# The rows of v of items 8 and 9 fetched two items later, in the step of their own value products

## Chip, cores, metric

The kernel runs on one core of a Trainium2 chip. The metric is the device time of one execution in microseconds (us).

## What is computed

Causal attention with a decay bias on 32 heads (4 batches of 8, 576 positions, head size 64), then a gated linear unit over the 2304 tokens with two more matrices behind it, then a soft mixture of 8 experts with 4 slots each:

```python
scores = scale * np.matmul(q, k.transpose(0, 1, 3, 2))
bias = -(cum[:, :, :, None] - cum[:, :, None, :])      # cum: running sum of max(s, 0)
scores = np.where(causal, -1e9, scores + np.minimum(bias, 0.0))
attn = softmax(scores)
x = (attn @ v), heads side by side                     # 2304 x 512
h = ((x @ w1) * (x @ w2)) @ w3 @ w_out                  # 2304 x 512
logits = h @ phi
slot_input = softmax over tokens(logits).T @ h
slot_out[e] = relu(slot_input[e] @ moe2_w1[e]) @ moe2_w2[e]
out = softmax over slots(logits) @ slot_out
```

All of it is float32; some matrices come as 64-bit floats and are converted on the chip ("words").

## The kernel before

**Items.** Attention is done in 40 items (ITEMS, L273). Items 0 to 7 are heads 0 to 7 with the query tiles 0 to 2, items 8 to 15 the same heads with the query tiles 3 and 4, items 16 to 39 the other heads with all five tiles. A block of tokens (BLK, L34) is 320 or 256 columns wide.

**Steps of an item.** att_steps (L646) writes the work of each step n: the scores of item n (att_scores, L330: products on TensorE into sc_ps, reduction by VectorE at L352, exponential by ScalarE at L357); in between, att_norm (L362, GpSimd) and the transposes (att_transpose, L374: pt_ps and ptd_ps on TensorE, copied to pt and ptd by ScalarE at L387 and L401) of item n-1; the fetches of what comes next; and, in even steps, the value products of the pair n-2 and n-1 (att_pv, L403: x_ps on TensorE at L110, copied at L434 and L435). Fetches for later items are issued in the list prep: v by att_values (L293) one item ahead, the decay rows by att_prep (L301) and q and k by att_fetch (L275) three and four items ahead.

**v.** One fetch brings the rows of v of a pair of heads and is made at the odd item; it serves both items of the pair. There are two buffers for v (VB = 2, L85), so a fetch waits until the value products of an earlier pair have read the buffer.

**Words.** The matrices w1 and w2 come as 64-bit words, 512 KB at a time, in 16 pieces named w12_i_e (fetch_words, L175; three buffers, NRAW = 3). ScalarE (L192) and VectorE (L195, L196, L199) convert each piece, then ScalarE (L223) and GpSimd (L224) split it for the GLU products (glu_half, L441: gl on TensorE at L447). Behind them come wot and w3t, which are multiplied with phi early (use_rows, L240).

**Order.** SyncE (SP) issues nearly all fetches, strictly in the order in which the program writes them, and stands at each until its buffer is free. The other engines run in orders that a scheduler makes when the program is built. weave (L685) mixes the lists of attention, GLU and words by their costs; a fetch counts nothing in it.

Of the kernel before, what the change touches and what calls it, by code (L numbers as in the profile page):

```python
# [22 lines left out]
B, H, S, D = 4, 8, 576, 64  # L23
# [24 lines left out]
def attn_glu_softmoe_kernel(  # L48
# [244 lines left out]
    def att_values(n, ap):  # L293
        h, tiles = ITEMS[n]
        if h % 2:
            vt = ap.tile([P, 9, 2, D], F32, tag="v", name=f"v_{n}", bufs=VB)
            nv = 2 * tiles[-1] + 1
            nc.sync.dma_start(vt[:, :nv], v[h // 2, :, :nv])
            hd[n]["v"] = hd[n - 1]["v"] = vt

    def att_prep(n, ap):  # L301
        h, tiles = ITEMS[n]
        t = hd[n]
        raw, q0, q1 = t["raw"], t["q0"], t["q1"]
        if n < NF32:
            rows = raw
        else:
            rows = ap.tile([P, 2, S], F32R, tag="qb", name=f"qb_{n}", bufs=QAB)
            qa = ap.tile([P, 2, S], F32R, tag="qa", name=f"qa_{n}", bufs=QAB)
        if n < NDIR:  # L310
            for a in range(2):
                nc.sync.dma_start(rows[64 + 2 * a : 66 + 2 * a, :, :q1].bitcast(F32), dec[a][h : h + 1, :, :, :q1])
        else:
            (nc.scalar if NF32 <= n < 24 else nc.sync).dma_start(rows[64:68, :, :q1].bitcast(F32), rows_d[h].rearrange("a b n t -> (a b) n t")[:, :, :q1])
        if n < NF32:
            t["mul"] = [rows[:68]]
            return
        rq, rk, qb = raw[:, 0], raw[:, 1], rows
        nc.vector.tensor_copy(qa[:, 0, q0:q1], rq[:, q0:q1])  # L319
        nc.scalar.dma_start(qb[0:64, 0, q0:q1].bitcast(F32), qa[0:64, 0, q0:q1].bitcast(F32))  # L320
        nc.vector.tensor_copy(qa[:, 1, :q1], rk[:, :q1])
        nc.gpsimd.tensor_tensor(  # L322
            out=qb[0:64, 1, :q1], in0=rk[0:64, :q1], in1=qa[0:64, 1, :q1].bitcast(F32), op=ALU.subtract
        )
        nc.gpsimd.tensor_tensor(  # L325
            out=qa[64:, 0, q0:q1], in0=rq[64:, q0:q1], in1=qa[64:, 0, q0:q1].bitcast(F32), op=ALU.subtract
        )
        t["mul"] = [qa, qb[:68]]

    def att_scores(n, i, ap):  # L330
        t, tiles = hd[n], ITEMS[n][1]
        if i == tiles[0]:
            t["nmax"] = sm.tile([P, 6], F32, tag="nmax", name=f"nmax_{n}")
            t["rsum"] = rsum_t[n % 3]
            if n >= H or n % 2 == 0:
                t["sc"] = ap.tile([P, 1600], F32, tag="sc", name=f"sc_{n}", bufs=SCB)
            else:
                t["sc"] = hd[n - 1]["sc"][:, 800:]
        nmax, rsum, mul = t["nmax"], t["rsum"], t["mul"]
        q0, r = QT[i]  # L340
        W = q0 + r

        r = P
        sc = t["sc"][:, 64 * i * i : 64 * i * i + W]
        cuts = [(0, W)] if W <= 512 else [(0, W // 2), (W // 2, W)]
        for m, (a, z) in enumerate(cuts):
            pp = psum("sg", f"sc_ps_{n}_{i}_{m}")
            for x in mul:
                nc.tensor.matmul(pp[:r, : z - a], x[:, 0, q0 : q0 + r], x[:, 1, a:z], start=x is mul[0], stop=x is mul[-1])  # L349
            m0 = S - P if i == 0 else S - W + a  # L350
            last = m == len(cuts) - 1
            nc.vector.tensor_tensor_reduce(  # L352
                out=sc[:r, a:z], in0=pp[:r, : z - a], in1=hd["mask"][:r, m0 : m0 + z - a], scale=-0.125,
                scalar=3.0e38 if m == 0 else nmax[:r, 5:6], op0=ALU.add, op1=ALU.min,
                accum_out=nmax[:r, i : i + 1] if last else nmax[:r, 5:6],
            )
        nc.scalar.activation(  # L357
            out=sc[:r, :W], in_=sc[:r, :W], func=AF.Exp, bias=nmax[:r, i : i + 1], scale=-1.0,
            accum_out=rsum[:r, i, 0:1],
        )  # L360

    def att_norm(n):  # L362
        t, tiles = hd[n], ITEMS[n][1]
        rinv = sm.tile([P, 5], F32, tag="rinv", name=f"rinv_{n}")
        span = slice(tiles[0], tiles[-1] + 1)
        nc.vector.tensor_reduce(out=rinv[:, span], in_=t["rsum"][:, span], axis=AX.X, op=ALU.add)
        nc.vector.reciprocal(rinv[:, span], rinv[:, span])  # L367
        for i in tiles:
            sc = t["sc"][:, 64 * i * i : 64 * i * i + sum(QT[i])]
            nc.gpsimd.tensor_scalar(  # L370
                out=sc, in0=sc, scalar1=rinv[:, i : i + 1], scalar2=1.0, op0=ALU.mult, op1=ALU.mult
            )

    def att_transpose(n, i, ap):  # L374
        t = hd[n]
        tiles = [j for j in ITEMS[n][1] if j]
        if i == tiles[0]:
            t["pt"] = ap.tile([P, 10, P], F32, tag="pt", name=f"pt_{n}", bufs=PTB)
            t["ptd"] = ap.tile([P, 5, 64], F32, tag="ptd", name=f"ptd_{n}", bufs=PTB)
        pt, ptd = t["pt"], t["ptd"]  # L380
        W = sum(QT[i])
        sc = t["sc"][:, 64 * i * i : 64 * i * i + W]
        tp = psum("tp", f"pt_ps_{n}_{i}")
        for j in range(i):
            nc.tensor.transpose(tp[:, j * P : (j + 1) * P], sc[:, j * P : (j + 1) * P], ident)  # L385
        p0, step = PT[i]
        t["turned", i] = nc.scalar.copy(  # L387
            out=pt[:, p0 : p0 + step * (i - 1) + 1 : step], in_=tp[:, : i * P].rearrange("p (j q) -> p j q", q=P)
        )
        if i == tiles[-1]:  # L390


            dg = psum("tp", f"ptd_ps_{n}")
            own = [j for j in ITEMS[n][1] if j] + [0] * (ITEMS[n][1][0] == 0)
            for k in [len(own) - 1, *range(len(own) - 2, -1, -1)]:
                j = own[k]
                c0 = max(0, 64 * j * j + sum(QT[j]) - P)
                p0 = 64 * k + (64 if j == 0 else 0)
                nc.tensor.transpose(dg[:, p0 : p0 + P], t["sc"][:, c0 : c0 + P], ident)  # L399
                t["diag", j] = k  # L400
            t["turned", "d"] = nc.scalar.copy(out=ptd[:, : len(own)].rearrange("p j q -> p (j q)"), in_=dg[:, 64 : 64 * len(own) + 64])  # L401
# [244 lines left out]
    def att_steps(ap):  # L646

        groups = [[] for _ in range(B + 1)]
        N = len(ITEMS)
        for n in range(N + 1):  # L650
            tiles = ITEMS[n][1] if n < N else ()
            old = [i for i in ITEMS[n - 1][1] if i] if 0 < n <= N else []
            sc = [(0.2 + 0.3 * i, lambda i=i, n=n: att_scores(n, i, ap)) for i in tiles]
            tr = [(0.2 + 0.3 * i, lambda i=i, n=n: att_transpose(n - 1, i, ap)) for i in old]
            norm = [(0, lambda n=n: att_norm(n - 1))] if 0 < n <= N else []
            prep = [(0, lambda n=n: att_values(n + 1, ap))] if n + 1 < N else []
            d = FAR if n + FAR < NF32 else 1 if NF32 <= n + 1 < N else 0
            if d:
                prep += [(0, lambda m=n + d: att_prep(m, ap))]
            d = FAR + 1 if n + FAR + 1 < NF32 else 2 if NF32 <= n + 2 < N else 0  # L660
            if d:
                prep += [(0, lambda m=n + d: att_fetch(m, ap))]
            blks = [k for k in range(2) if BLK[k][2][0] in ITEMS[n - 1][1]]
            pv = [(1.4, lambda n=n, k=k: att_pv(n - 2, k)) for k in blks] if n > 0 and n % 2 == 0 else []
            groups[min(B, max(0, (n - 1) // H))] += [
                *sc[:1], *norm, *sc[1:2], *prep, *sc[2:3], *tr[:1], *sc[3:4], *tr[1:2], *sc[4:], *tr[2:], *pv
            ]
        return groups

# [77 lines left out]
    with tc.tile_pool(name="att", bufs=1) as ap:  # L747
# [14 lines left out]
        hd["mask"] = mask  # L762
        hd["ap"] = ap
        att = att_steps(ap)
        decay_rows()
        for n in range(NDIR):
# [20 lines left out]
        def load(k):  # L787
            i = k // 2 - 1
            if FC <= i < N0:
                (sum_rows if k % 2 else use_rows)(*TODO[i])  # L790
            if k < 2 * N0:
                load_words(k, ap)
            if k + NRAW < 2 * N0:
                fetch_words(k + NRAW, ap)
# [8 lines left out]
        prep = [(1, lambda k=k: load(k)) for k in range(2 * N0 + 2)]  # L803
# [15 lines left out]
        for b in range(2, B):  # L819
            steps, late = glu_steps(b - 1, late)  # L820
            n = len(more) // (B - b)
# [309 lines left out]
```

## Time and profile before

| | |
|---|---|
| median of 3 runs | 555.44 us (553.01 to 556.08) |
| profiled execution | 556.72 us, of which the span from first to last instruction 554.9 us |
| TensorE (PE) busy | 519.0 us, 94% |
| VectorE (DVE) busy | 316.0 us, 57% |
| ScalarE (ACT) busy | 311.5 us, 56% |
| GpSimd (POOL) busy | 199.2 us, 36% |
| moved by DMA | 118.03 MB, mean 213 GB/s |
| mean granted TensorE clock | 0.977 |

The table reads as averages over stages that differ. Steps 8 to 12, of which the change speaks, run between about 43 and 85 us.

### The profile page before, as it was taken

To read this page: it belongs to the slowest core of one execution; us is meant where nothing else is said; L and a number is where in the kernel's file an instruction comes from. 1 tells how busy PE (TensorE), PEld (TensorE's weight loads), DVE (VectorE), ACT (ScalarE), POOL (GpSimd) and SP (SyncE) were. 2 spreads that over 40 slices of the span, in tenths; PEclk is the share of its full clock that TensorE was granted. 3 is DMA by queue.
4 is the path that set the end of the run, shared out by engine and by line. 5 is a ranking of instruction groups with operands and counts; after the bars stand their busy time and mean duration, and the time that the engine had idled before them with its cause. 6 is when DMAs were issued, how large, how long until landed. Compare 5 with 4: busy or idle time off the path is not lost.

```text
span 554.9 us, 11841 instructions
## 1 busy us (share of the span) xinstructions
PE 519.0 (94%) x4288; PEld 436.2 (79%) x4288; DVE 316.0 (57%) x966; ACT 311.5 (56%) x845; POOL 199.2 (36%) x247
## 2 busy tenths in 40 slices
PE   3899799999889999999999899999999999999993
PEld 2667588888778898999989799898989999853452
DVE  7568677789865383866457677446641311243433
ACT  4576667688876674865687577557743211321222
POOL 5474463628764474343433444334220000000000
PEclk9997979999799999999999999999999999999998
DMA  5766953977572251654657347454403999689977
GB/s 153 246 164 181 284 186 135 305 289 252 180 254 98 77 189 40 206 174 154 194 170 231 128 150 222 130 170 131 153 33 119 406 409 388 238 297 424 420 288 242
DMA packets 38809, 118.03 MB, mean 213 GB/s; under 512 B 4224, under 2 KB 10560, under 8 KB 35296
## 3 DMA queue, kind: packets, MB, share of 16 engines
q1 hardware_dynamic: 36768, 113.60, 59.7%
q10 hardware_dynamic: 1984, 3.69, 2.5%
q8 instruction: 34, 0.56, 0.4%
q14 instruction: 23, 0.19, 0.1%
HBM read 102.11 MB, written 11.60 MB: 205 GB/s over the span
## 4 chain that ended last, share of the span: by engine, by line
PE 74%; DMA 9%; DVE 8%; issue 3%; ACT 2%; SPq 1%; POOL 1%; DVEq 0%; ACTq 0%; POOLq 0%
PE gl L447 33%; PE x_ps L110 8%; PE sc_ps L349 8%; PE pt_ps L385 5%; DMA raw_w<-in_w 4%; PE gn_ps L617 3%; PE o_ps L1032 3%; DMA raw<-in_qk 3%; PE h_ps L994 3%; PE ptd_ps L399 3%; PE z_ps L110 2%; DVE w3t L204 1%; PE lg L110 1%; DVE sc L352 1%; DVE w_w L204 1%
## 5 line engine op out<-in xcount | busy, mean ns | idle before, releaser
L447 PE MATMUL gl<-x,w12t 128*128 128x320 f32 (+1 forms) x1536 | 240.0, 306 | 0.5 <-DVE gT L465 0.3
L447 PEld LDWEIGHTS gl<-x,w12t 128*128 128x128 f32 x1536 | 214.9, 192 | 8.3 <-issue 4.6
L370 POOL TENSOR_SCALAR sc<-sc,rinv 128x64 f32<-128x64 f32 (+4 forms) x160 | 95.8, 615 | 47.5 <-DVE rinv L367 32.9
L357 ACT ACTIVATE sc<-sc,nmax 128x64 f32<-128x64 f32 (+4 forms) x160 | 89.8, 563 | 34.6 <-DVE nmax L352 34.2
L325 POOL TENSOR_TENSOR qa<-raw,qa 64x576 fp32r<-64x576 f32 x24 | 36.4, 1516 | 136.9 <-DVE qa L319 111.3
L352 DVE CUSTOM_DVE_ANT_0 sc<-sc_ps,mask 128x64 f32<-128x64 f32 (+4 forms) x160 | 64.5, 422 | 31.7 <-PE sc_ps L349 28.0
L387 ACT COPY pt<-pt_ps 128x128 f32<-128x128 f32 (+3 forms) x128 | 53.1, 424 | 36.0 <-PE pt_ps L385 21.7
L385 PE MATMUL pt_ps<-ident,sc 128*128 128x128 f32 x320 | 55.8, 285 | 5.8 <-ACT pt L387 2.6
L349 PE MATMUL sc_ps<-qa 128*128 128x64 f32 (+1 forms) x144 | 46.6, 336 | 6.3 <-DVE nmax L352 3.3
L385 PEld LDWEIGHTS pt_ps<-ident,sc 128*128 128x128 f32 x320 | 38.5, 144 | 15.9 <-issue 7.2
L453 ACT COPY a<-gl 128x256 f32<-128x256 f32 (+1 forms) x64 | 25.5, 400 | 43.9 <-PE gl L447 38.0
L110 PE MATMUL x_ps<-pt,v 128*64 128x256 f32 (+1 forms) x384 | 47.6, 361 | 0.0
L349 PE MATMUL sc_ps<-raw 68*128 68x288 f32 (+4 forms) x96 | 35.4, 513 | 11.3 <-DMA raw<-rows 9.6
L349 PE MATMUL sc_ps<-qb 68*128 68x64 f32 (+1 forms) x144 | 44.0, 310 | 0.0
L1003 POOL MEMSET ht<- 128x1024 f32 x2 | 1.9, 954 | 108.0 <-DVE ew L907 99.1
L110 PEld LDWEIGHTS x_ps<-pt,v 128*64 128x64 f32 x384 | 33.1, 142 | 6.8 <-issue 1.3
L322 POOL TENSOR_TENSOR qb<-raw,qa 64x576 fp32r<-64x576 f32 x24 | 37.5, 1564 | 2.2 <-PE gn_ps L617 0.5
L349 PEld LDWEIGHTS sc_ps<-qa 128*128 128x128 f32 x144 | 27.9, 194 | 9.8 <-DVE nmax L352 4.6
L435 DVE TENSOR_TENSOR x<-x_ps,x 128x320 fp32r<-128x320 f32 (+1 forms) x32 | 13.9, 450 | 37.9 <-ACT x L434 37.9
L349 PEld LDWEIGHTS sc_ps<-raw 68*128 68x128 f32 x96 | 21.2, 258 | 16.1 <-issue 12.3
L192 ACT ACTIVATE w_w<-raw_w 128x512 f32<-128x512 f32 x32 | 21.7, 678 | 18.5 <-DMA raw_w<-in_w 18.4
L357 ACT ACTIVATION_READ_ACCUMULATOR sc<-sc,nmax 128x1 f32 x160 | 31.0, 194 | 0.0
(180 smaller groups left out, 782.5 us busy)
## 6 DMA issues: line engine op xcount, KB each, us to landing
ew<-in_ew SPq DMA_DIRECT2D x27, 1024.0 KB
raw_w<-in_w SPq DMA_DIRECT2D x32, 512.0 KB
raw<-in_qk SPq DMA_DIRECT2D x24, 576.0 KB
v<-in_v SPq DMA_DIRECT2D x16, 576.0 KB
raw_w3t<-in_w3t SPq DMA_DIRECT2D x16, 512.0 KB
raw_wot<-in_wot SPq DMA_DIRECT2D x8, 512.0 KB
raw_wo<-in_wo SPq DMA_DIRECT2D x8, 512.0 KB
w_d<-w_w SPq DMA_DIRECT2D x8, 512.0 KB
```

The source lines that it names most:

```text
L110: mm = nc.tensor.matmul(out_, lhs, rhs, start=start, stop=stop)
L192: line_up(nc.scalar.activation(out=w, in_=hi.bitcast(F32), func=AF.Copy, scale=F64_SCALE))
L322: nc.gpsimd.tensor_tensor(out=qb[0:64, 1, :q1], in0=rk[0:64, :q1], in1=qa[0:64, 1, :q1].bitcast(F32), op=ALU.subtract)
L325: nc.gpsimd.tensor_tensor(out=qa[64:, 0, q0:q1], in0=rq[64:, q0:q1], in1=qa[64:, 0, q0:q1].bitcast(F32), op=ALU.subtract)
L349: nc.tensor.matmul(pp[:r, : z - a], x[:, 0, q0 : q0 + r], x[:, 1, a:z], start=x is mul[0], stop=x is mul[-1])
L352: nc.vector.tensor_tensor_reduce(out=sc[:r, a:z], in0=pp[:r, : z - a], in1=hd["mask"][:r, m0 : m0 + z - a], scale=-0.125, scalar=3.0e38 if ...
L357: nc.scalar.activation(out=sc[:r, :W], in_=sc[:r, :W], func=AF.Exp, bias=nmax[:r, i : i + 1], scale=-1.0, accum_out=rsum[:r, i, 0:1],)
L370: nc.gpsimd.tensor_scalar(out=sc, in0=sc, scalar1=rinv[:, i : i + 1], scalar2=1.0, op0=ALU.mult, op1=ALU.mult)
L385: nc.tensor.transpose(tp[:, j * P : (j + 1) * P], sc[:, j * P : (j + 1) * P], ident)
L387: t["turned", i] = nc.scalar.copy(out=pt[:, p0 : p0 + step * (i - 1) + 1 : step], in_=tp[:, : i * P].rearrange("p (j q) -> p j q", q=P))
L447: nc.tensor.matmul(acc[:, :nt], w12_t[fc][:, wi, n, kc], x_t[b, blk, kc][:, xi], start=k == 0, stop=k == 3 * KC - 1)
L453: st["a_copy"] = nc.scalar.copy(out=a_sb[:, :nt], in_=acc[:, :nt])
```

## The change

The fetch of v_9, the rows of v for the items 8 and 9, was written in step 8, among the fetches ahead. It is now written in step 10, behind the transposes of item 9 and right ahead of the value products of items 8 and 9 (H is 8).

```diff
-            prep = [(0, lambda n=n: att_values(n + 1, ap))] if n + 1 < N else []
+            prep = [(0, lambda n=n: att_values(n + 1, ap))] if n + 1 < N and n + 1 != H + 1 else []
+            vals = [(0, lambda n=n: att_values(n - 1, ap))] if n - 1 == H + 1 else []
...
-                *sc[:1], *norm, *sc[1:2], *prep, *sc[2:3], *tr[:1], *sc[3:4], *tr[1:2], *sc[4:], *tr[2:], *pv
+                *sc[:1], *norm, *sc[1:2], *prep, *sc[2:3], *tr[:1], *sc[3:4], *tr[1:2], *sc[4:], *tr[2:], *vals, *pv
```

**SP.** Names are tile_item or tile_matrix_piece_half, with a running number at the end; raw is q and k, and from rows_d the decay rows, of an item. Before, from the words w12_4_1 on:

```order
L178 DMA raw_w12_4_1_558<-in_w12 128x512
L298 DMA v_9_579<-in_v 128x1152
L314 DMA raw_11_529<-rows_d_101 4x1152
L287 DMA raw_12_583<-in_qk 64x256
L288 DMA raw_12_583<-in_qk 64x576
L178 DMA raw_w12_5_0_607<-in_w12 128x512
L811 DMA phi_sb_105<-in_phi 128x128
L178 DMA raw_w12_5_1_670<-in_w12 128x512
L314 DMA raw_12_583<-rows_d_101 4x1152
L287 DMA raw_13_673<-in_qk 64x256
L288 DMA raw_13_673<-in_qk 64x576
L178 DMA raw_w12_6_0_721<-in_w12 128x512
```

After the change these rows are the same but without the second, and v_9 stands here:

```order
L178 DMA raw_w12_6_0_704<-in_w12 128x512
L298 DMA v_11_733<-in_v 128x1152
L314 DMA raw_13_671<-rows_d_101 4x1152
L287 DMA raw_14_737<-in_qk 64x256
L288 DMA raw_14_737<-in_qk 64x576
L178 DMA raw_w12_6_1_765<-in_w12 128x512
L298 DMA v_9_782<-in_v 128x1152
L178 DMA raw_w12_7_0_827<-in_w12 128x512
```

v_9 moved behind v_11 and the words w12_6_1. v_11 now takes the buffer of v_5 and v_9 that of v_7; from v_13 on each waits for the same value products as before. One other fetch moved on SP: q and k of item 17 stood ahead of the words wot_3_1 and now stand behind them, since the lists that weave mixes have one entry less and one more.

**ScalarE.** The conversions of the words 5_0, 5_1 and 6_0 (L192), between the copies of transposes (L387, L401) and the exponentials (L357). Before:

```order
L223 CAST w12t_4_662<-w_w12_4_0_663 128x512
L401 COPY ptd_6_537<-ptd_ps_6_545 128x192
L387 COPY pt_7_586<-pt_ps_7_1_588 128x128
L223 CAST w12t_4_662<-w_w12_4_1_714 128x512
L387 COPY pt_7_586<-pt_ps_7_2_591 128x2x128
L401 COPY ptd_7_587<-ptd_ps_7_595 128x192
L192 ACTIVATE w_w12_5_0_760<-raw_w12_5_0_607 128x512
L357 ACTIVATE sc_10_694,rsum_1_94<-sc_10_694,nmax_10_693 128x448
L387 COPY pt_8_676<-pt_ps_8_3_678 128x3x128
L434 CAST x_0_0_3_251<-x_ps_6_0_609 128x320
L192 ACTIVATE w_w12_5_1_817<-raw_w12_5_1_670 128x512
```

After:

```order
L223 CAST w12t_4_660<-w_w12_4_0_661 128x512
L192 ACTIVATE w_w12_5_0_758<-raw_w12_5_0_605 128x512
L401 COPY ptd_6_537<-ptd_ps_6_545 128x192
L387 COPY pt_7_584<-pt_ps_7_1_586 128x128
L223 CAST w12t_4_660<-w_w12_4_1_697 128x512
L387 COPY pt_7_584<-pt_ps_7_2_589 128x2x128
L192 ACTIVATE w_w12_5_1_820<-raw_w12_5_1_668 128x512
L401 COPY ptd_7_585<-ptd_ps_7_593 128x192
L357 ACTIVATE sc_10_692,rsum_1_94<-sc_10_692,nmax_10_691 128x448
L192 ACTIVATE w_w12_6_0_878<-raw_w12_6_0_704 128x512
L223 CAST w12t_5_757<-w_w12_5_0_758 128x512
L387 COPY pt_8_674<-pt_ps_8_3_676 128x3x128
```

The three conversions moved ahead of two to five copies each.

**TensorE.** The value products of items 8 and 9 (x_ps_8_1), which read v_9. Before, the first stands ahead of the GLU products gl_0_0_1_1, the other eleven behind them and ahead of gl_0_0_2_0:

```order
L399 MATMUL ptd_ps_9_755<-ident_86,sc_9_630 128x128 x2
L349 MATMUL sc_ps_11_4_0_810<-raw_11_529 128x288
L349 MATMUL sc_ps_11_4_1_813<-raw_11_529 128x288
L110 MATMUL x_ps_8_1_784<-pt_8_676,v_9_579 64x256
L447 MATMUL gl_0_0_1_1_826<-x_0_0_0_111,w12t_1_316 128x320 x3
L447 MATMUL gl_0_0_1_1_826<-x_0_0_1_155,w12t_1_316 128x320 x3
L447 MATMUL gl_0_0_1_1_826<-x_0_0_2_179,w12t_1_316 128x320 x3
L447 MATMUL gl_0_0_1_1_826<-x_0_0_3_251,w12t_1_316 128x320 x3
L110 MATMUL x_ps_8_1_784<-pt_9_742,v_9_579 64x256
```

After:

```order
L399 MATMUL ptd_ps_9_753<-ident_86,sc_9_628 128x128 x2
L349 MATMUL sc_ps_11_4_0_834<-raw_11_529 128x288
L349 MATMUL sc_ps_11_4_1_837<-raw_11_529 128x288
L447 MATMUL gl_0_0_2_0_862<-x_0_0_0_111,w12t_2_431 128x320 x3
L447 MATMUL gl_0_0_2_0_862<-x_0_0_1_155,w12t_2_431 128x320 x3
L447 MATMUL gl_0_0_2_0_862<-x_0_0_2_179,w12t_2_431 128x320 x3
L447 MATMUL gl_0_0_2_0_862<-x_0_0_3_251,w12t_2_431 128x320 x3
L385 MATMUL pt_ps_10_3_847<-ident_86,sc_10_692 128x128 x3
L110 MATMUL x_ps_8_1_784<-pt_8_674,v_9_782 64x256
L110 MATMUL x_ps_8_1_784<-pt_9_740,v_9_782 64x256
```

All twelve value products now stand behind gl_0_0_2_0 (and gl_0_0_1_1 stands ahead of ptd_ps_9). The first product with wot, wot_ps_0, stood with the value products of items 12 and 13 and now stands with those of items 10 and 11.

## Rows read from the trace of the kernel before

**Rows 1.** Busy time by stretch: us, busy by engine (instructions), clock, DMA share, GB/s.

```profile
49.00:50.00 1.00, 1.00 (x6) 0.49 (x5) 1.00 (x4) 0.56 (x2) 1.00 (x2) 0.50 0.00 0
...
55.00:60.00 5.00, 4.42 (x41) 3.56 (x40) 2.41 (x6) 2.42 (x6) 3.42 (x3) 1.00 0.95 275
...
70.00:75.00 5.00, 5.00 (x21) 3.95 (x22) 3.29 (x10) 3.30 (x8) 1.41 (x1) 0.50 0.35 119
...
80.00:90.00 10.00, 10.00 (x60) 8.43 (x59) 7.42 (x22) 8.32 (x20) 4.63 (x4) 1.00 0.54 191
```

**Rows 2.** SP's queue in order of time: start, duration (us), line, transfer.

```profile
45.31 0.33 SPq L178 DMA_DIRECT2D raw_w<-in_w  x1
51.75 0.33 SPq L298 DMA_DIRECT2D v<-in_v  x1
...
53.73 0.52 SPq L178 DMA_DIRECT2D raw_w<-in_w  x1
...
54.86 0.34 SPq L178 DMA_DIRECT2D raw_w<-in_w  x1
...
57.28 0.34 SPq L178 DMA_DIRECT2D raw_w<-in_w  x1
...
62.64 3.45 SPq L178 DMA_DIRECT2D raw_w<-in_w  x2
...
76.29 0.33 SPq L298 DMA_DIRECT2D v<-in_v  x1
...
101.69 0.38 SPq L290 DMA_DIRECT2D raw<-in_qk  x1
103.02 0.33 SPq L178 DMA_DIRECT2D raw_wot<-in_wot  x1
```

**Rows 3.** The chain of waits in order of time: start, us, what.

```profile
19.09 3.87 DMA raw_w<-in_w
...
57.28 8.56 DMA raw_w<-in_w
```

**Rows 4.** ACT in order of time; in brackets the idle time before and its end.

```profile
54.63 0.32 ACT L401 COPY ptd<-ptd_ps 128x192 f32<-128x192 f32 x1 [0.46 <-PE ptd_ps L399]
...
58.96 0.67 ACT L192 ACTIVATE w_w<-raw_w 128x512 f32<-128x512 f32 x1 [1.75 <-DMA raw_w<-in_w]
...
62.12 0.66 ACT L192 ACTIVATE w_w<-raw_w 128x512 f32<-128x512 f32 x1 [1.16 <-DMA raw_w<-in_w]
...
65.92 0.67 ACT L192 ACTIVATE w_w<-raw_w 128x512 f32<-128x512 f32 x1 [1.38 <-DMA raw_w<-in_w]
```

**Rows 5.** DVE in order of time: the last step on words 3_1, 4_0 and 4_1.

```profile
45.57 1.64 DVE L199 SCALAR_TENSOR_TENSOR w_w<-raw_w,w_w 128x512 uint32<-128x512 uint32 x1
...
50.17 1.65 DVE L199 SCALAR_TENSOR_TENSOR w_w<-raw_w,w_w 128x512 uint32<-128x512 uint32 x1
...
54.93 1.12 DVE L199 SCALAR_TENSOR_TENSOR w_w<-raw_w,w_w 128x512 uint32<-128x512 uint32 x1
```

**Rows 6.** PE in order of time (runs of equal instructions merged).

```profile
63.40 0.52 PE L385 MATMUL pt_ps<-ident,sc 128*128 128x128 f32 x3 [1.56 <-ACT pt L387]
...
66.89 0.63 PE L385 MATMUL pt_ps<-ident,sc 128*128 128x128 f32 x4 [1.33 <-ACT ptd L401]
...
70.15 3.57 PE L447 MATMUL gl<-x,w12t 128*128 128x320 f32 x12
73.65 2.16 PE L110 MATMUL x_ps<-pt,v 128*64 128x256 f32 x12
...
76.93 2.01 PE L447 MATMUL gl<-x,w12t 128*128 128x320 f32 x12
78.77 1.89 PE L349 MATMUL sc_ps<-raw 68*128 68x448 f32 x6
...
90.83 1.51 PE L110 MATMUL x_ps<-pt,v 128*64 128x256 f32 x12
...
104.67 0.64 PE L110 MATMUL wot_ps<-wot,phi_sb 128*32 128x256 f32 x8
```

## Prediction

> **What bounds it now.** I read the busy times by stretch first, then SyncE's queue (SP) in order of time, then what ACT, VectorE (DVE) and TensorE (PE) waited for in the same stretch, and last the chain of waits. Over the whole span TensorE is the bound, so a gain has to come from places where PE stands idle or runs at half clock, and the reader should look for one such place near the moved fetch.
>
> It is there. Between 49 and 50 us the DMA engines move nothing [rows 1], though much is waiting to be fetched. SP says why: after the words w12_4_1 at 45.31 its next instruction, the fetch of v_9, starts at 51.75 [rows 2]. The two buffers for v are taken, v_9 needs the one that v_5 holds, and it stands there until the value products of items 4 and 5 are done on PE. SP runs strictly in order, so 6 us of other fetches stand behind it. They then come in one crowd: words 5_0, 5_1 and 6_0 go out at 53.73, 54.86 and 57.28 [rows 2], the DMA engines are full from 55 on (a share of 0.95, 275 GB/s) [rows 1], and ACT waits for each landing, until 58.96, 62.12 and 65.92 [rows 4]. ACT also copies PE's transposes out of PSUM, in order behind those conversions, so PE stands 1.56 us before 63.40 and 1.33 us before 66.89 [rows 6]. The chain of waits agrees: one link, the fetch of words from 57.28, is 8.56 us long [rows 3]. After the two gaps the granted clock in 70 to 75 is 0.50 [rows 1], the lower of its two levels, 1.2 GHz.
>
> **The change, part by part.**
>
> *The wait of v_9 on SP goes.* In the new order the rows behind it run through. Next late is the buffer of each words fetch (three in rotation), free when DVE has made its last step on the words three before: 45.57 + 1.64 = 47.2, 50.17 + 1.65 = 51.8 and 54.93 + 1.12 = 56.05 [rows 5]. So words 5_0, 5_1 and 6_0 go out 6.5, 3.0 and 1.2 us earlier than before [rows 2], and into an empty queue. An earlier words fetch, at 19.09, with little ahead of it took 3.87 us to land [rows 3], which puts the landings near 51.1, 55.7 and 59.9, against 58.96, 62.12 and 65.92 [rows 4]: 8, 6 and 6 us earlier. The first two come before ACT reaches them; for the third ACT stands about 1 us.
>
> *What PE gets back.* The two gaps, 1.56 + 1.33 = 2.89 us. Then the slow clock behind them: twelve GLU products took 3.57 us at the lower level and take 2.01 at the full one, twelve value products 2.16 against 1.51 [rows 6], together 1.56 + 0.65 = 2.21. Sum 5.1 us. Other work of that slow stretch (score products) I leave uncounted as a reserve.
>
> *What it costs there.* ACT and DVE now have the conversions of 5_0, 5_1 and 6_0 ahead of the copies of transposes and of the score reductions that PE needs. A conversion takes 0.67 us on ACT [rows 4]. Bounds: nothing, if PE has other work then; 2 us, if all three delay PE in full. I take one, 0.7, since PE has GLU products and value products to do between those copies. Remains 5.1 - 0.7 = 4.4.
>
> *The fetch of v_9 itself.* It now stands behind v_11 and words 6_1. v_11 takes the buffer of v_5 and v_9 that of v_7, both free by then. Words 6_1 wait for the conversion of 5_0: before, they went out at 62.64 [rows 2], 3.7 us after it began on ACT at 58.96 [rows 4]. It now stands ahead of the copy of ptd_6, which was at 54.63 [rows 4], so words 6_1 go out near 59 and v_9 near 60. From 56 on, words 6_0, v_11, q and k of item 14, words 6_1 and v_9 are 512 + 576 + 208 + 512 + 576 KB = 2.44 MB; at 275 GB/s [rows 1] that is 8.9 us, to 65, and about 2 us of tail (3.87 less the 1.9 that 512 KB take at that rate) gives a landing near 67. PE now comes to these products after twelve more GLU products: the scores of item 12 began at 78.77 [rows 6], now 4.4 earlier at 74.4, and about 3 us of value products and a transpose stand ahead of them, so PE needs v_9 near 71.4. The late bound: words 6_1 still go out at 62.64 [rows 2] and take the 8.56 us of the crowded fetch [rows 3], to 71.2, and 576 KB more take 2.1 us, to 73.3. So PE's exposed wait lies between nothing and 1.9 us; I take nothing, since the queue is drained at 56 this time, and have 4 us to spare. DMA issues themselves are as many as before.
>
> *v_13.* It takes v_9's buffer and waits at SP's head as before, then until 76.29 [rows 2], when PE's value products of items 8 and 9 had ended. Those now begin near 71.4 and take some 2.5 us, so SP's next wait ends near 74, over 2 us earlier. The wot words behind it keep pace with PE, roughly.
>
> *One more swap.* The q and k of item 17 now stand behind words wot_3_1 and go out after 103.02 instead of at 101.69 [rows 2], under 2 us later. PE's scores of item 17 stand far behind the 104.67 row in its order: nothing.
>
> *Afterwards.* PE is busy for 10.00 of the 10 us from 80 to 90 [rows 1], and so in the two windows after it, with no wait there that could swallow a gain; what it has gained by 75 it keeps. The orders of PE, ACT and DVE differ from before for about the first third of the program; I set no sum for that and widen the range by it.
>
> The profiled execution was 556.72 us, 1.3 above the median of 555.44. 556.72 - 4.4 = 552.3 in its own terms; on the median, **551.0 us**.
>
> **The rivals.**
>
> *The words were not the limit (no change).* For: 6_0 goes out only 1.2 us earlier, its buffer being held by DVE, and it is the link of the chain. Against: the queue ahead of it is empty this time. If ACT still waits 2 us or so for 6_0 or 6_1, one gap of over 1.3 us stays and the slow clock with it: 2.21 is lost again, and of 2.89 about half. Gain 1.4: 554.
>
> *v_9 is late (no change).* The fetch gives up all its lead, and its landing decides when PE goes on, since PE is in order and all its later work stands behind. At the late bound of 73.3, with PE there at 71.4, PE stands 1.9 us, and a half-clock stretch as in 70 to 75 follows, 2.21 more. That takes back 4.1 of 4.4: 555. For the rule: v_9 is issued about 8 us later than before; against it: 4 us to spare in the sum above. The Trainium skill, page "DMA: Bandwidth & Descriptors", section "Rules for kernel authors", says the same as a general rule: issue a DMA early, compute, and wait on its semaphore late; by that alone this change is the wrong way round. The 6 us that SP stood at v_9 speak against that rule here: an early place in an in-order queue is early only if its buffer is free.
>
> *v_13 comes later (slower).* PE now does twelve GLU products ahead of these value products, 2.01 us [rows 6]. If PE gains nothing before them, they end at 76.3 + 2.0, and SP, which waits for them with v_13, holds the four wot words 2 us longer. The first product with wot, at 104.67 before [rows 6], now stands beside the value products of items 10 and 11 (90.83 before [rows 6]), so its cover of 14 us is gone: PE waits the 2 us there, with a slow stretch of 2.21 behind. 555.4 + 4.2 = 559.6. It decides if the value products of items 8 and 9 end later than 76.3.
>
> *That the change doesn't do what it says:* the order shows v_9's row moved, so no.
>
> **How the numbers follow.** A measurement of this kernel tells about 0.5% (2.8 us) from no change. Forecast, gain of 3 to 6 us: 0.64. Words not the limit: 0.16. v_9 late: 0.10. v_13 later: 0.10. Faster by over 0.5% is the first, 0.64; within it the two middle ones, 0.26; slower 0.10. Range: down to 548 (all 5.1 kept, 550.3, less the 2.4 by which the lowest run of before lies under its median), up to 556.5 (v_9 late, with one more PE gap as long as the longest of before, 1.56 [rows 6]); the slower case is left out.
>
> **What would show it.** Right: SP issues words 5_0 near 47 with no wait at v before it; no second without DMA traffic near 49; ACT's waits for words together under 2 us between 55 and 70 (1.75 + 1.16 + 1.38 = 4.3 before [rows 4]); PE's gaps near 63 and 66 gone, clock 1.0 from 60 to 80; scores of item 12 near 74.4. Wrong: a PE gap at the value products of items 8 and 9 ended by the DMA of v, a clock of 0.5 anywhere from 60 to 80, or the scores of item 12 at 74 and the span still near 555, which would mean that the gain is given back in the reordered part.

## The result and the profile after

The changed kernel took 560.64 us (median of 12 runs, 556.96 to 565.77) against 555.12 us (12 runs, 551.27 to 559.7) for the kernel before: a ratio of 1.012, 95% interval 1.0094 to 1.0146. It is slower by 1.2%; the forecast was 551.0. Ratios here leave out disturbed runs, so that one can differ from that of two medians, and where they differ the ratio counts.

The profiled execution took 556.96 us (span 555.1), the fastest of the twelve; a second one, taken later, took 562.42 and is used below. Columns are those of the rows of before.

Busy time by stretch, after:

```profile
45.00:50.00 5.00, 5.00 (x39) 3.92 (x40) 4.93 (x15) 3.70 (x11) 2.89 (x3) 1.00 1.00 304
49.00:50.00 1.00, 1.00 (x19) 0.93 (x15) 0.96 (x4) 0.76 (x4) 1.00 (x2) 1.00 1.13 271
55.00:60.00 5.00, 2.79 (x15) 1.52 (x15) 4.86 (x9) 3.13 (x8) 2.43 (x2) 0.78 0.83 251
60.00:65.00 5.00, 5.00 (x32) 4.88 (x33) 4.83 (x10) 3.06 (x7) 2.45 (x2) 0.54 0.88 256
70.00:75.00 5.00, 5.00 (x45) 4.18 (x43) 4.74 (x12) 3.88 (x9) 1.33 (x2) 1.00 0.05 20
```

SP's queue, after (words 5_0, 5_1, 6_0; v_9; v_13):

```profile
47.91 0.52 SPq L178 DMA_DIRECT2D raw_w<-in_w  x1
...
51.68 0.33 SPq L178 DMA_DIRECT2D raw_w<-in_w  x1
...
54.97 0.34 SPq L178 DMA_DIRECT2D raw_w<-in_w  x1
...
62.05 0.33 SPq L298 DMA_DIRECT2D v<-in_v  x1
...
75.18 0.33 SPq L298 DMA_DIRECT2D v<-in_v  x1
```

ACT's first conversion steps of words 5_0 and 5_1, after:

```profile
53.84 0.67 ACT L192 ACTIVATE w_w<-raw_w 128x512 f32<-128x512 f32 x1 [0.83 <-DMA raw_w<-in_w]
...
56.13 0.67 ACT L192 ACTIVATE w_w<-raw_w 128x512 f32<-128x512 f32 x1 [0.32 <-DMA raw_w<-in_w]
```

The queue does what was forecast. The hole without traffic at 49 is gone (DMA busy, 271 GB/s, against 0 in [rows 1]), the words go out at 47.91, 51.68 and 54.97 against 53.73, 54.86 and 57.28 [rows 2], and ACT begins on 5_0 and 5_1 at 53.84 and 56.13 against 58.96 and 62.12 [rows 4]. In the chain of waits the link of 8.56 us at 57.28 [rows 3] is gone; the longest transfer in it ahead of 250 is now

```profile
155.86 7.76 DMA raw<-in_qk
```

PE does not profit. In order of time, after:

```profile
54.86 0.41 PE L385 MATMUL pt_ps<-ident,sc 128*128 128x128 f32 x2 [1.09 <-ACT ptd L401]
...
58.58 1.33 PE L349 MATMUL sc_ps<-raw 68*128 68x288 f32 x2 [2.10 <-DVE nmax L352]
...
73.18 1.74 PE L110 MATMUL x_ps<-pt,v 128*64 128x256 f32 x16
...
75.57 1.89 PE L349 MATMUL sc_ps<-raw 68*128 68x448 f32 x6
...
109.02 0.44 PE L399 MATMUL ptd_ps<-ident,sc 128*128 128x128 f32 x2 [1.03 <-ACT pt L387]
110.51 0.64 PE L110 MATMUL wot_ps<-wot,phi_sb 128*32 128x256 f32 x8 [1.05 <-DVE x L435]
...
122.95 2.29 PE L447 MATMUL gl<-x,w12t 128*128 128x256 f32 x9 [1.23 <-DVE gC L465]
```

The gaps of 1.56 and 1.33 us [rows 6] are gone, and the value products of items 8 and 9 begin at 73.18 without a wait for v. In their place stand 1.09 and 2.10 us a little earlier, the second with a clock of 0.54 behind it in 60 to 65; then 1.03, 1.05 and 1.23 us between 109 and 123, where before PE stood nowhere for half a microsecond. The scores of item 12 begin at 75.57, 3.2 us ahead of 78.77 [rows 6]; by 130 that lead is lost. (Two more profiles of the kernel before, in experiment 5, have these scores at 71.45 and 72.47, so that against them the change is late here already.)

### The profile page after: what moved, and what is told of

Read it like the earlier page. It is cut to its first block, busy times and chain, and to the rows that moved or that the text cites. A ratio compares the mean times of both kernels' runs of the same rounds, so it can differ in the third digit from the quotient of the medians.

```text
span 555.1 us, 11842 instructions
## 1 busy us (share of the span) xinstructions
PE 516.3 (93%) x4288; PEld 434.1 (78%) x4288; DVE 317.2 (57%) x966; ACT 313.9 (57%) x845; POOL 198.3 (36%) x247
## 4 chain that ended last, share of the span: by engine, by line
PE 63%; DVE 3%; DMA 3%; ACT 1%; issue 1%; POOL 0%; DVEq 0%; SPq 0%; ACTq 0%
PE gl L447 29%; PE x_ps L110 6%; PE sc_ps L349 5%; PE pt_ps L385 4%; PE gn_ps L617 3%; PE o_ps L1033 3%; PE h_ps L995 3%; PE z_ps L110 2%; PE ptd_ps L399 2%; DMA raw<-in_qk 1%; PE lg L110 1%; DMA raw_w<-in_w 1%; PE y_ps L919 1%; DMA out<-ot 1%; PE out_ps L1057 1%
## 5 line engine op out<-in xcount | busy, mean ns | idle before, releaser
L447 PE MATMUL gl<-x,w12t 128*128 128x320 f32 (+1 forms) x1536 | 236.6, 304 | 3.3 <-DVE gC L465 1.2
L370 POOL TENSOR_SCALAR sc<-sc,rinv 128x64 f32<-128x64 f32 (+4 forms) x160 | 92.8, 597 | 60.3 <-DVE rinv L367 48.6
L357 ACT ACTIVATE sc<-sc,nmax 128x64 f32<-128x64 f32 (+4 forms) x160 | 89.7, 562 | 29.9 <-DVE nmax L352 29.1
L325 POOL TENSOR_TENSOR qa<-raw,qa 64x576 fp32r<-64x576 f32 x24 | 36.5, 1519 | 128.7 <-DVE qa L319 103.1
L387 ACT COPY pt<-pt_ps 128x128 f32<-128x128 f32 (+3 forms) x128 | 53.1, 425 | 31.1 <-PE pt_ps L385 20.7
L110 PEld LDWEIGHTS x_ps<-pt,v 128*64 128x64 f32 x384 | 34.3, 149 | 7.6 <-issue 3.5
L435 DVE TENSOR_TENSOR x<-x_ps,x 128x320 fp32r<-128x320 f32 (+1 forms) x32 | 14.0, 451 | 37.9 <-ACT x L434 37.9
L224 POOL TENSOR_TENSOR w12t<-w_w,w12t 128x512 fp32r<-128x512 f32 x16 | 24.3, 1525 | 18.3 <-ACT w12t L223 18.3
L357 ACT ACTIVATION_READ_ACCUMULATOR sc<-sc,nmax 128x1 f32 x160 | 30.8, 192 | 0.0
```

The costliest lines, as they stand in the source:

```text
L110: mm = nc.tensor.matmul(out_, lhs, rhs, start=start, stop=stop)
L224: nc.gpsimd.tensor_tensor(out=tl, in0=w, in1=th.bitcast(F32), op=ALU.subtract)
L325: nc.gpsimd.tensor_tensor(out=qa[64:, 0, q0:q1], in0=rq[64:, q0:q1], in1=qa[64:, 0, q0:q1].bitcast(F32), op=ALU.subtract)
L357: nc.scalar.activation(out=sc[:r, :W], in_=sc[:r, :W], func=AF.Exp, bias=nmax[:r, i : i + 1], scale=-1.0, accum_out=rsum[:r, i, 0:1],)
L370: nc.gpsimd.tensor_scalar(out=sc, in0=sc, scalar1=rinv[:, i : i + 1], scalar2=1.0, op0=ALU.mult, op1=ALU.mult)
L387: t["turned", i] = nc.scalar.copy(out=pt[:, p0 : p0 + step * (i - 1) + 1 : step], in_=tp[:, : i * P].rearrange("p (j q) -> p j q", q=P))
```

## Experiments

The change does two things at once: it moves a fetch on SP, and, because the scheduler works from the order in which the program is written, it gives PE, ACT, DVE and GpSimd new orders for the first third. To part them, some kernels below have the engines' orders pinned: after the program has been written, each instruction of these four engines is tied behind the one that precedes it in a stored list.

```diff
         attn_glu_softmoe_kernel(tc, *args)
+        _pin(tc, nc)
...
+    for e, ks in perm.items():
...
+        for a, b in zip(seq, seq[1:]):
+            tc.add_manual_dep(b, a.name, dep, reason="pinned")
```

All ratios are to the kernel before on the same chip, with their 95% intervals.

### 1. The fetch alone: fetch_only

```diff
-            prep = [(0, lambda n=n: att_values(n + 1, ap))] if n + 1 < N else []
+            prep = [(0, lambda n=n: att_values(n + 1, ap) if n + 1 != H + 1 else None)] if n + 1 < N else []
...
-            pv = [(1.4, lambda n=n, k=k: att_pv(n - 2, k)) for k in blks] ...
+            late = lambda n: att_values(n - 1, ap) if n - 1 == H + 1 else None
+            pv = [(1.4, lambda n=n, k=k: (late(n), att_pv(n - 2, k))) for k in blks] ...
+        _pin(tc, nc)
```

The stored lists are the orders of the kernel before.

> v_9 is fetched late, as in the change, but the orders of PE, ACT, DVE and GpSimd are held to those of the kernel before, instruction for instruction; q and k of item 17 keep their old place too. Theory O (the reordered engines lose the time, the fetch itself gains or does nothing): no slower than before, a ratio of 0.99 to 1.00. Theory F (the late fetch loses it, by what SyncE does behind it): a ratio near 1.012, as the change. If both have a share, in between.

Measured: 0.9995 (0.9964 to 1.0026), 553.18 against 553.89 us. Not slower, so theory F falls; but no gain either. It also shows that the pinning by itself costs nothing that these runs could tell. PE, in this kernel, at the value products of items 8 and 9:

```profile
66.98 0.65 PE L110 MATMUL x_ps<-pt,v 128*64 128x256 f32 x2 [2.32 <-DMA v<-in_v]
```

Under the old orders PE comes to these products sooner than v_9 does, and stands 2.32 us. That is the rival "v_9 is late". Its price was 1.9 us of waiting and 2.21 of half clock behind it; the wait is here, the half clock is not (1.00 from 60 to 80).

### 2. The orders alone: order_only

```diff
+            first = lambda n: att_values(n + 1, ap) if n + 1 == H + 1 else None
...
-                prep += [(0, lambda m=n + d: att_prep(m, ap))]
+                prep += [(0, lambda n=n, m=n + d: (first(n), att_prep(m, ap)))]
...
+        _pin(tc, nc)
```

The stored lists are the orders of the changed kernel. The lists of steps keep the changed kernel's lengths, by an empty entry, so that the weaving and item 17's fetch are those of the change.

> The other corner: PE, ACT, DVE and GpSimd run in the order of the changed kernel, instruction for instruction, q and k of item 17 stand where the change puts them, and v_9 alone is fetched at its old place, so SyncE stands at it again near 46 to 52 us. Theory O: slower than before by 1.2% or more (1.012 to 1.02, since the words come late again on top). Theory F: as before, 0.997 to 1.003.

Measured: 1.0139 (1.0082 to 1.0197). The new orders cost the whole of it, with v_9 fetched where it always was. A part of the 1.4% is this kernel's own: SP stands at v_9 again, until 51.73, ACT waits 3.96 us for words 5_0, and PE stands 3.99 us before 59.49, ended by ACT's copy at L401 behind their conversion.

### 3. The change again, and the same fetch under two other orders

changed_again is the changed kernel, unedited; v9_no_shift is the kernel of experiment 1 without the pinning; only_swap is that of experiment 2 without it (v_9 at its old place, only the lengths of the lists as in the change).

> The changed kernel itself, beside the others on the same chip: 1.012 again, and a second profile, which tells whether the places where the first one lost time (PE standing at 109 to 111, a half clock from 120 to 130) are there each time.

> v_9 is fetched late in the same step, but from within an existing entry of the step's list, so the list lengths, the weaving of the steps and the place of q and k of item 17 stay as before; the scheduler orders the engines itself (on PE about half as many rows differ from before as with the change). Theory O: somewhere from 0.99 to 1.02, not the same as the change, since it is another order. Theory F: 1.012, as the change.

> v_9 is fetched at its old place; the lists of steps have the lengths of the changed kernel, which shifts the weaving by a step and puts q and k of item 17 behind words wot_3_1; the scheduler orders the engines (some 250 rows of PE differ from before). If the shift and the late item 17 carry the loss: 1.006 to 1.012. If they carry none: 0.997 to 1.003. Theory G: 1.004 to 1.012.

Measured: changed_again 1.0105 (1.0062 to 1.0147); v9_no_shift 1.0092 (1.0062 to 1.0123); only_swap 1.0094 (1.0057 to 1.0131). only_swap does not move v_9 at all, and loses nearly as much as the change. The second profile of the change has the same gaps at the same instructions: 2.09 us at 59.42, 1.34 at 112.30, 1.06 at 113.79 and 1.23 at 127.70.

Where the time goes, by the moment at which ACT casts the value products of three pairs of items (line 434), in profiles of single executions:

| kernel | orders | items 8, 9 | items 14, 15 | items 24, 25 | span |
|---|---|---|---|---|---|
| before (the profile of the prediction) | old | 76.30 | 127.10 | 246.07 | 554.9 |
| before, second look | old | 72.71 | 124.19 | 243.44 | 552.2 |
| before, third look | old | 73.23 | 123.72 | 242.48 | 551.4 |
| fetch_only | old | 71.86 | 123.16 | 240.83 | 549.5 |
| the change | new | 76.13 | 129.65 | 247.15 | 555.1 |
| changed_again | new | 77.18 | 134.36 | 251.35 | 560.6 |
| order_only | new | 81.44 | 135.01 | 252.41 | 562.1 |

From the last cast to the end all of them take 308 to 310 us: the loss lies wholly ahead of it. From 40 to that cast (columns as in [rows 1]) in the change, changed_again, fetch_only and fix_more, the last of which comes in experiment 4:

```profile
40.00:247.15 207.15, 195.71 (x1609) 169.03 (x1607) 149.33 (x424) 145.65 (x386) 107.61 (x118) 0.96 0.59 192
40.00:251.35 211.35, 198.54 (x1612) 170.91 (x1612) 149.71 (x424) 145.78 (x389) 108.16 (x118) 0.95 0.58 188
40.00:240.83 200.83, 189.45 (x1604) 162.70 (x1601) 152.12 (x423) 144.19 (x388) 107.00 (x115) 1.00 0.59 194
40.00:243.68 203.68, 190.84 (x1607) 164.13 (x1605) 149.61 (x423) 143.72 (x386) 109.40 (x118) 1.00 0.61 193
```

PE is idle for 10.2 and 8.8 us in the two later looks at before, at a mean clock of 0.97 and 0.98, and for 11.4, 12.8 and 14.9 us in the change, changed_again and order_only, at 0.96, 0.95 and 0.97. But idle time alone does not part the orders: fetch_only, which is level with before, has 11.4 us of it at a clock of 1.00. The clock says more. Over the runs that the ratios count, its mean over the whole program is 0.990 to 0.991 for before, 0.981 and 0.982 for the change, 0.979 for order_only. An estimate from these means, if the clock is 0.5 or 1.0: about 11 us at half clock in before (2 x 0.010 x 552), 20 in changed_again and 23 in order_only. Each of these costs half a microsecond of PE's work, so that some 4.5 of the 5.9 us lost in changed_again and 6 of the 8.5 in order_only would be half clock.

### 4. What is wrong with the new orders

Two of the places, in the second profile of the change. First DVE ahead of PE's gap at 59.42 (a chain of conversion steps of words 4_1 and 5_0, then the reduction of the scores of item 10 that PE waits for):

```profile
53.58 1.00 DVE L196 SCALAR_TENSOR_TENSOR w_w<-raw_w,w_w 128x512 int32<-128x512 int32 x1
54.62 1.12 DVE L199 SCALAR_TENSOR_TENSOR w_w<-raw_w,w_w 128x512 uint32<-128x512 uint32 x1
55.66 1.48 DVE L195 TENSOR_SCALAR w_w<-w_w 128x512 int32<-128x512 int32 x1
57.18 1.64 DVE L196 SCALAR_TENSOR_TENSOR w_w<-raw_w,w_w 128x512 int32<-128x512 int32 x1
58.75 0.61 DVE L352 CUSTOM_DVE_ANT_0 sc<-sc_ps,mask 128x448 f32<-128x448 f32 x1
...
111.50 1.90 DVE L207 SCALAR_TENSOR_TENSOR wot<-raw_wot,wot 128x512 int32<-128x512 int32 x1
113.32 0.41 DVE L435 TENSOR_TENSOR x<-x_ps,x 128x256 fp32r<-128x256 f32 x1
```

PE made the first of those scores from 51.12 on. In the order of before their reduction stands ahead of L195 of words 5_0; here two conversion steps stand ahead of it, and both are long while GpSimd works beside them:

```profile
55.17 3.10 POOL L224 TENSOR_TENSOR w12t<-w_w,w12t 128x512 fp32r<-128x512 f32 x2
...
111.36 1.50 POOL L325 TENSOR_TENSOR qa<-raw,qa 64x576 fp32r<-64x576 f32 x1 [1.40 <-DVE qa L319]
```

Second, ACT near 110. It stands 1.95 us for words wot_3_1 and then 1.39 us at a transfer of its own, whose source DVE casts only behind those words; the copy that PE waits for is queued behind both:

```profile
108.87 0.69 ACT L192 ACTIVATE wot<-raw_wot 128x512 f32<-128x512 f32 x1 [1.95 <-DMA raw_wot<-in_wot]
...
111.76 0.48 ACT L387 COPY pt<-pt_ps 128x384 f32<-128x384 f32 x1 [1.39 <-DVE qa L321]
```

Each time a conversion stands ahead of something that PE is about to need. The next kernels put pieces of the changed kernel's orders right and pin the rest. The rows that move are these: a plus is where a row of an engine's order now stands, a minus where it stood.

fix_scores, DVE: the reductions of item 10's scores ahead of the conversion of words 5_0.

```diff
+L352 sc_10<-sc_ps_10_3_0
+L352 sc_10<-sc_ps_10_4_0
 L195 w_w12_5_0
 L196 w_w12_5_0
-L352 sc_10<-sc_ps_10_3_0
-L352 sc_10<-sc_ps_10_4_0
```

fix_item17, SP, DVE and ACT one after the other:

```diff
+L290 raw_17<-in_qk
 L178 raw_wot_3_1<-in_wot
-L290 raw_17<-in_qk
...
+L319 qa_17<-raw_17
+L321 qa_17<-raw_17
 L465 gC_0_0_5
...
-L319 qa_17<-raw_17
-L321 qa_17<-raw_17
...
+L320 qb_17<-qa_17
 L192 wot_3<-raw_wot_3_1
...
-L320 qb_17<-qa_17
```

fix_all has both and this, on DVE:

```diff
+L465 gC_0_0_7
 L207 w3t_1<-raw_w3t_1_0
-L465 gC_0_0_7
```

> The changed kernel with the first of the three pieces alone (the two score reductions of item 10 ahead of the conversion of words 5_0). Theory Q: PE's gap of 2.1 us near 59 shrinks to under 0.7, and the half clock behind it goes: about 3 us, 1.005 to 1.007. Theory D: 1.009 to 1.012.

> The changed kernel with the second piece alone (item 17's q and k, their casts and the transfer on ACT ahead of the conversion of words wot_3_1). Theory Q: ACT no longer stands 1.4 us at that transfer and PE's gaps of 1.3 and 1.1 us near 112 go: 2 to 4 us, 1.004 to 1.007. Theory D: 1.009 to 1.012.

> The changed kernel with three pieces of its new order put right, everything else held instruction for instruction: on VectorE two score reductions of item 10 ahead of the conversion of words 5_0; q and k of item 17 ahead of words wot_3_1 on SyncE, with their two casts on VectorE and the transfer that ACT issues for them ahead of the conversion of those words; on VectorE the GLU product of chunk 7 ahead of one step of a words conversion. Theory Q (the new order loses its time where a conversion stands ahead of something that PE waits for, at these three places): the PE gaps of 2.1, 1.3 and 1.1, and 1.2 us are gone and the ratio falls from 1.011 to 0.995 to 1.002. Theory D (the loss is spread over the whole reordered part): it stays at 1.006 to 1.012.

Measured: fix_scores 1.0111 (1.0067 to 1.0155), fix_item17 1.0181 (1.0132 to 1.023), fix_all 1.0066 (1.003 to 1.0102). By these numbers neither of the first two pieces alone gives anything back, and both of theory Q's forecasts for them fail: fix_scores and fix_all lie in theory D's range, fix_item17 above either. (These three kernels ran beside before, not beside the changed kernel, whose ratios are 1.012 and 1.0105.) In fix_scores the gap of 2.09 us is gone, and those near 109 (1.22 and 1.06 us) and 125 (1.22) stand as they were. In fix_item17 ACT's stand at its transfer is gone, and PE's wait at wot_ps has grown from 1.06 to 1.87 us, since DVE's subtraction at L435 is still behind the conversion. If anything is recovered, it is by the three together, and their interval still meets that of changed_again. So two pieces more.

fix_more has all of fix_all and these, first on ACT, then on DVE:

```diff
+L434 x_0_1_2<-x_ps_12_1
+L387 pt_14<-pt_ps_14_3
 L192 wot_3<-raw_wot_3_1
 L203 raw_wot_3_1
-L434 x_0_1_2<-x_ps_12_1
...
-L387 pt_14<-pt_ps_14_3
...
+L435 x_0_1_2<-x_ps_12_1
 L204 wot_3<-raw_wot_3_1
...
-L435 x_0_1_2<-x_ps_12_1
...
+L435 x_0_1_3<-x_ps_14_1
 L207 w3t_2<-raw_w3t_2_1
-L435 x_0_1_3<-x_ps_14_1
...
+L352 sc_18<-sc_ps_18_1_0
 L204 w3t_3<-raw_w3t_3_0
 L207 w3t_3<-raw_w3t_3_0
-L352 sc_18<-sc_ps_18_1_0
```

> The changed kernel with the three pieces put right and two more: the cast and the subtraction of the value products of items 12 and 13, and the first copy of transposes of item 14, ahead of the conversion of words wot_3_1 on ACT and DVE; the subtraction of items 14 and 15 and one score reduction of item 18 ahead of a words conversion on DVE. If the loss sits where conversions stand ahead of what PE waits for, each piece gives back 1 to 2 us more: 1.000 to 1.004. If putting one right only moves the wait to the next: 1.005 to 1.009, as with three pieces.

Measured: 1.0021 (0.9987 to 1.0055). A dozen instructions put ahead of conversions (one is a fetch, put ahead of one of words), with PE's order untouched, bring the changed kernel level with before; the interval lies clear of those of the change, though up to 0.55% of a loss may be left. So it is not the amount of work, nor v_9's fetch, nor PE's own order, but which small copies and reductions stand behind which conversions on ACT and DVE, at several places together. That is shown for the dozen as a whole; what each piece is worth is not.

The path from these orders to the time is less simple than a sum of gaps. In its profile fix_more is idle for 12.8 us from 40 to the last cast, no less than the change (11.4 and 12.8), but at a clock of 1.00 against 0.96 and 0.95, and over its runs the clock is 0.990. What the dozen gave back is half clock in the main. Gaps of 1.0 to 1.6 us are still there, with no half clock behind them; why one gap has it behind it and another not is not shown by these runs. Two that are left, in PE's order of fix_more:

```profile
83.13 2.02 PE L447 MATMUL gl<-x,w12t 128*128 128x320 f32 x12 [1.02 <-ACT a L453]
...
109.12 1.87 PE L447 MATMUL gl<-x,w12t 128*128 128x320 f32 x11 [1.57 <-DVE nmax L352]
```

The first can be read back to v_13 (no experiment of its own). SP stands at it until the value products of items 8 and 9 are done, and the wot words stand behind it. Here it went out at 72.76 and the words from 73.58; in a later look at before at 68.96 and from 71.63. ACT waits 1.50 us for them in this kernel, 2.88 us in changed_again, 0.36 in that look.

### 5. Why the freed queue is worth so little

The same fetch, four transfers later instead of fifteen (the expectations count its own row too and say five and sixteen): behind words 5_0, ahead of words 5_1, whose buffer is held until about 52 anyway. The orders of before are pinned.

```diff
-            prep = [(0, lambda n=n: att_values(n + 1, ap))] if n + 1 < N else []
+            prep = [(0, lambda n=n: att_values(n + 1, ap) if n != H else None)] if n + 1 < N else []
+            late = lambda n: att_values(n + 1, ap) if n == H else None
...
+            pv = [(1.4, lambda n=n, k=k: (late(n), att_pv(n - 2, k))) for k in blks] ...
+        _pin(tc, nc)
```

row_free is the same without the last line, with orders that the scheduler makes.

> All orders as in the kernel before, but v_9 stands only five rows later on SyncE, behind words 5_0 and ahead of words 5_1, which are held by their buffer until about 52 us anyway. Theory S (SyncE's 6 us at v_9 do cost PE time, and the late v_9 took the gain back): PE's wait of 2.32 us for v_9, seen with the fetch sixteen rows later, is gone, words 5_0 still go out near 48, and the ratio is 0.990 to 0.995. Theory N (the words were not what PE stood for in a usual execution): 0.997 to 1.003.

> The same kernel as the one with v_9 five rows later under the old orders, which had a median 2.5 us under that of before in its runs but a ratio of 0.9997. If freeing SyncE is worth something, the median lies 2 to 4 us below again and the ratio at 0.993 to 0.998; if it is worth nothing, both are level within 1.5 us.

> v_9 five rows later as well, but the orders of PE, ACT, DVE and GpSimd are left to the scheduler, which moves some 330 rows of PE's order. If any reordering of this tuned order costs time (theory G, general): 1.004 to 1.012. If only the order that comes with the fetch at the value products is bad (theory P, particular): 0.990 to 1.003.

Measured: row_later 0.9997 (0.9965 to 1.003), row_later_again 0.9962 (0.9933 to 0.9991), row_free 1.0066 (1.0034 to 1.0099). The first comparison is level and speaks for theory N, the second is 0.4% faster; the median of 2.5 us under before in the first is not borne out by its ratio. So this version is faster than the change, and at best slightly faster than before. The same fetch with the orders left to the scheduler is slower: all four orders that the scheduler made anew here (the change, v9_no_shift, only_swap, row_free) cost 0.7 to 1.2%, so theory G holds as far as they go.

In row_later SP stands 1.3 us at v_9 (until 49.77), at a time when words 5_1 would be held by their buffer anyway, and PE's value products follow without a wait:

```profile
47.93 0.52 SPq L178 DMA_DIRECT2D raw_w<-in_w  x1
...
49.77 0.33 SPq L298 DMA_DIRECT2D v<-in_v  x1
...
51.56 0.33 SPq L178 DMA_DIRECT2D raw_w<-in_w  x1
```

```profile
63.86 0.65 PE L110 MATMUL x_ps<-pt,v 128*64 128x256 f32 x2
...
70.86 1.89 PE L349 MATMUL sc_ps<-raw 68*128 68x448 f32 x6
```

The scores of item 12 begin at 70.86, 7.9 us ahead of 78.77 [rows 6], more than the 4.4 forecast, and yet the ratios are 0.9997 and 0.9962. So the kernel before was profiled twice more, with no edit.

> The kernel before itself, for a second profile. If the two PE gaps near 63 and 67 (1.56 and 1.33 us, ended by ACT behind words) and the half clock behind them stand in every execution, they are here again and the freed queue should have been worth the whole 5 us; if they were partly an accident of the one profile, they are smaller or gone, and the 2 to 3 us that v_9 five rows later brought is all there was.

> A third profile of the kernel before, for the same question: the sum of the two PE gaps near 63 and 67 and the granted clock from 70 to 75.

SP and PE of the kernel before, second look:

```profile
49.15 0.33 SPq L298 DMA_DIRECT2D v<-in_v  x1
```

```profile
55.97 0.52 PE L385 MATMUL pt_ps<-ident,sc 128*128 128x128 f32 x3 [1.51 <-ACT pt L387]
...
60.67 0.52 PE L385 MATMUL pt_ps<-ident,sc 128*128 128x128 f32 x3
...
65.02 2.02 PE L447 MATMUL gl<-x,w12t 128*128 128x320 f32 x12
...
71.45 0.92 PE L349 MATMUL sc_ps<-raw 68*128 68x448 f32 x2
```

Third look:

```profile
49.73 0.33 SPq L298 DMA_DIRECT2D v<-in_v  x1
```

```profile
61.68 0.52 PE L385 MATMUL pt_ps<-ident,sc 128*128 128x128 f32 x3 [0.57 <-ACT pt L387]
...
66.04 2.03 PE L447 MATMUL gl<-x,w12t 128*128 128x320 f32 x12
...
72.47 1.89 PE L349 MATMUL sc_ps<-raw 68*128 68x448 f32 x6
```

Busy time from 45 to 50 in the first profile, the second and the third look:

```profile
45.00:50.00 5.00, 5.00 (x20) 3.79 (x18) 4.57 (x12) 3.30 (x9) 2.52 (x3) 0.50 0.48 153
45.00:50.00 5.00, 4.44 (x39) 3.53 (x37) 4.97 (x14) 4.27 (x11) 2.74 (x3) 1.00 0.58 172
45.00:50.00 5.00, 4.93 (x41) 3.97 (x40) 4.96 (x17) 4.30 (x13) 2.30 (x3) 1.00 0.77 264
```

v_9 goes out at 49.15 and 49.73, not at 51.75; of the two gaps that the sum was made of, one of 0.57 us is left in one look (before 61.68) and none in the other (60.67); the twelve GLU products take 2.02 and 2.03 us, not 3.57; and the scores of item 12 begin at 71.45 and 72.47. In the first profile PE ran at half clock from 45 to 50 (0.50, against 1.00 in both looks). The rows read so: the value products of items 4 and 5 ended some two microseconds later for it, so SP stood longer, the words came in a tighter crowd, and PE stood for them (the half clock itself was not an experiment).

The looks are not without gaps, though: both have one of 1.51 us near 56, where the first profile has 0.44, and one of 1.1 to 1.2 near 75. From the scores that begin at 43.54, 43.38 and 44.52 to those of item 12, PE is idle for 3.5, 2.3 and 2.3 us and busy for 31.8, 25.8 and 25.7, with equal work, at a mean clock of 0.81, 1.00 and 1.00. Some 6 of the 7 us by which the first profile is later are thus half clock, and only 1.2 idle time.

Against the two looks (single executions of 553.98 and 553.14 us), row_later is ahead by 0.6 and 1.6 us at the scores of item 12 in this profile, and in that of row_later_again, where they begin at 73.29, not at all. How the 0.4% of row_later_again comes about is therefore not shown; what the freed queue is worth lies between nothing and the 0.7% at the far end of that interval.

## Why the prediction was wrong

- **SyncE's wait goes: right.** Words 5_0, 5_1 and 6_0 at 47.2, 51.8 and 56.05 by the sum, 47.91, 51.68 and 54.97 measured; ACT's waits 0.83 and 0.32 us for the first two pieces and none to speak of for the third. "Into an empty queue" was not so: from 45 to 50 the DMA share is 1.00 (304 GB/s), and words 5_0 were in use at 53.84, 5.9 us after their issue, and not at 51.1; 5_1 at 56.13 (55.7).
- **"What PE gets back", 5.1 us: a mis-sized term.** All of it was read from the one profile of before, and the larger part was that execution's own, with its half clock at 45 to 50. In two other executions the two gaps come to 0 and 0.57 us with no half clock to speak of in 60 to 75 (0.99 and up), though they have gaps elsewhere. What the freed queue is worth was measured with old orders: nothing with v_9 fifteen transfers later (0.9995), nothing or 0.4% with it four later (0.9997 and 0.9962).
- **"What it costs there", 0.7 of at most 2 us: too small.** 1.09 and 2.10 us of PE gaps, ended by ACT and DVE, and a clock of 0.54 behind them. The bound counted a conversion as its 0.67 us on ACT; the longer gap was ended by DVE, where two steps of the conversion, 1.48 and 1.64 us in the second profile, stood ahead of the reduction. PE had no other products to do meanwhile: the next row of its order was a score product of item 10, and it stood there (58.58).
- **v_9 itself, nothing: right for the change, and in the main for the reason given.** PE came to these products later (73.18, by the sum 71.4), and by then the queue had drained (a DMA share of 0.05 from 70 to 75). That v_7's buffer would be free was wrong: v_9 stood at SP's head and went out at 62.05, not near 60, which cost nothing here. With the old order PE does wait, for 2.32 us, over the late bound of 1.9.
- **v_13 near 74, "over 2 us earlier": 75.18.** Earlier than 76.29 [rows 2], but 5 to 6 us later than the 68.96 and 69.98 of the other looks at before. The slower rival had this mechanism: it moved the cost to the wot words, and a wait of PE stands at that place indeed (0.45 us after, 1.71 us in changed_again), ended by ACT, not by wot_ps as the rival had it. It is at most a part of the loss: a wait of 1.02 us stands there in fix_more too, which is level with before.
- **The swap of item 17, nothing: not shown to cost.** ACT stood 1.39 us at its transfer, but taking that away alone gave nothing back.
- **The step that failed: "The orders of PE, ACT and DVE differ from before for about the first third of the program; I set no sum for that", with "what it has gained by 75 it keeps".** A term was put at nothing, without a reason, that was larger than all the others: 1.4% in order_only, some 8 us, where the forecast gain was 4.4. "Widen the range by it" was not done either: both bounds, 548 and 556.5, are worked out from other terms. The prediction named the sign to look for, scores of item 12 early and the span still near 555 (75.57 and 555.1 in the profile), but gave it no chance of its own, and 10% to slower in all, for another mechanism.

What stays open: which rule of the scheduler writes these orders, which of the dozen rows carry the loss, why the clock falls behind some gaps and not behind others, and whether some reordering by the scheduler would gain; of the four tried, none did.

## What to carry to other kernels

If a scheduler orders the engines, moving one transfer in the source is two edits, and the second one can be the larger: compare the orders, look at what now stands behind long conversions on ACT and DVE, and test the fetch with the old orders pinned before judging it. Count the half clock beside the idle time: by the figures above it was most of the difference here, between kernels (an estimate) and between executions of one kernel. A stall that is read from one execution may be that execution's own; look for a half clock ahead of it, and take a second profile before counting the gaps behind it as a gain. And where an in-order queue stands at a blocked transfer, move the transfer only so far as the next one that is blocked anyway: four places brought 0 and 0.4% in two comparisons and no wait on PE, fifteen brought nothing, with a wait of 2.32 us.

## What the runs showed of the hardware

VectorE's steps on words last 0.69 us (L196, L207) and 0.43 us (L195) by themselves, and up to 1.64, 1.90 and 1.48 us where GpSimd's products of two tiles (L224, L325) run beside them, as in the rows of experiment 4. The Trainium skill, page "SBUF — State Buffer", section "Who interferes with whom", says that a VectorE instruction with two inputs in SBUF contends with a GpSimd instruction that reads SBUF; the rows agree for L196 and L207. So an order that puts conversions beside GpSimd's work can make a step two to three and a half times as long. This is read from traces; no run changed GpSimd's work alone.
